# Narrower Q, K weight loads, joined rest loads and a re-ordered first stage in a conditioned attention and MLP block

## The chip, the cores and the metric

The kernel runs on one core of one Trainium2 chip. The metric is device microseconds of one execution, the median of the runs shown. TensorE (PE) multiplies matrices, VectorE (DVE), ScalarE (ACT) and GpSimd (POOL) do elementwise work, and SyncE (SP) issues nearly all DMAs. A DMA is carried out by 16 DMA engines; in this text the row of work that waits at one of them is called a ring.

## The reference, cut to what matters

```
def _A_ref(x, wqkv, wo):                 # S 2048, D 448, H 16, Dh 28
    qkv = (x @ wqkv).reshape(B, S, 3, H, Dh).transpose(2, 0, 3, 1, 4)
    ...                                   # each position attends to 8 positions, 2 apart, back from itself
    return o.transpose(0, 2, 1, 3).reshape(B, S, D) @ wo
def _B_ref(x, w1, b1, w2, b2):           # F 1792
    y = _layernorm(x)
    return gelu(y @ w1 + b1) @ w2 + b2
mod = (silu(c) @ w_mod).reshape(1, 6, 1, -1)
sa, ca, ga, sb, cb, gb = (mod[:, i] for i in range(6))
h = _layernorm(x) * (1 + ca) + sa
x = x + ga * _A_ref(h, wqkv, wo)
h = _layernorm(x) * (1 + cb) + sb
x = x + gb * _B_ref(h, w1, b1, w2, b2)
```

All inputs are bf16. `c` has 448 numbers, `w_mod` is 448 by 2688, `wqkv` 448 by 1344.

## The kernel before, in words

The 2048 tokens lie in eight tiles of 256 (128 partitions, two tokens each), `x_all[:, p]`. The depth 448 is cut into three full k-tiles of 128 rows and a **rest** of 64 rows. A rest uses half of the PE's rows, so the kernel keeps two copies or two halves of each rest weight, one on partitions 0 to 63 and one on 64 to 127, and loads them with two DMAs of 64 rows: `wm_r` (rest of the modulation's columns for `sa` and `ca`), `wqr_st` (rest of the Q and K weights, twice the same rows) and the last k-tile of `Wv` (rest of V, twice the same rows).

The first stage runs so. PE multiplies dummy weights (`warm_w`) while the first loads come. `c` is spread over partitions, silu is made from it (`e_c`, `silu_bf`, then a broadcast copy `silu_bc`), and PE multiplies `wm_st`, `wm_r` and `wm_d` (a copy of columns of both, laid twice) with it; two DVE additions make `mod_col`. Meanwhile tile 0 is normalised (`zy`) and transposed on PE (`ptr`), and `hT` is made of `ptr` and `mod_col`. The loaded Q and K weights are spread from 28 to 32 columns per head by copies on ACT, DVE and POOL (`Wqk` for the three k-tiles, `Wqr` for the rest), and PE forms Q and K of tiles 0 and 1 from `hT`, `Wqk` and `Wqr`: first what the full k-tiles give, then the rest. `spread` reads 4 columns past the last head, so the loads before are 900 columns wide (2 D + 4).

Tiles 2 to 7 go another way ("turns"): their `zy` is transposed by DMA (`zT`), and their Q and K are formed in natural order straight from `wqk_st` and `wqr_st`. Then come attention in 9 batches, the output projection, the second normalisation and the MLP, with attention and MLP interleaved in three phases. The second part of the modulation (`wmod`, four loads, 1.5 MB in all) is needed by the PE product `pb`, from which the output projection's scale comes.

Every task has a number; the string `ORDER` lists the numbers in the order in which the instructions are written, which is the order on each engine and on SP's queue, with `:A`, `:D`, `:P` where another engine than the usual one takes it and `+n@m` for n dummy products. `SLOTS` gives the buffers. SP issues the DMAs in program order with eight semaphores in turn, so each issue also waits for the DMA eight before it.

Of the kernel before, what the change touches and what calls it, by code (L numbers as in the profile page):

```python
# [66 lines left out]
487 401 490 454 403 402 436 453 455 370 444 404 434 371:D 456 372 491 457 488 405 459 493 458 460 445 492 435 494 461  # L67
# [86 lines left out]
def kernel(  # L154
# [68 lines left out]
    silu_bf = cst.tile([128, KT], BF16, name="silu_bf")  # L223
# [11 lines left out]
    wqk_st = sb("hm", [128, KT - 1, 2 * D + HP - DH], BF16, "wqk_st")  # L235
    wqr_st = sb("h2", [128, 2 * D + HP - DH], BF16, "wqr_st")
# [9 lines left out]
    def dconst(us, fn, writes):  # L246
        early.append(add("DVE", us, fn, writes=writes, after=[one], name="const " + writes[0]))
# [22 lines left out]
    dconst(0.06, lambda: nc.vector.memset(neg_half[:], -0.5), ["neg_half"])  # L270
# [83 lines left out]
    load_rest(0)  # L354
    load_rest(1)
    load_x(2, 4)
# [30 lines left out]
    def c_cols():  # L387
# [8 lines left out]
    add("DVE", 0.08, lambda: nc.vector.tensor_tensor(out=silu_bf[:], in0=e_c[:], in1=psc.t[:, 0, 0:128 * KT:128], op=ALU.mult),  # L396
        reads=["e_c"], bufs=[psc], writes=["silu"], name="silu")
    add("ACT", 0.18, lambda: nc.scalar.copy(out=silu_bc[:], in_=silu_bf[:].unsqueeze(2).to_broadcast([128, KT, HP])),
        reads=["silu"], writes=["silu_bc"], name="silu_bc")
# [32 lines left out]
    def spread(half):  # L432
# [3 lines left out]
        for ks in [[k] for k in range(KT - 1)]:  # L436
            k0, n = ks[0], len(ks)
            dst, src = (lambda k0=k0, n=n: Wqk[:, k0:k0 + n, half]), (lambda k0=k0, n=n: heads(wqk_st.t[:, k0:k0 + n, half * D:half * D + D], H))
            add("DVE", 0.06 + 0.18 * n, lambda dst=dst, src=src: nc.vector.tensor_copy(out=dst(), in_=src()), reads=[f"wqk{k}" for k in ks],
                bufs=[wqk_st], writes=[f"W{half}{k}" for k in ks], port=True, name="spread",  # L440
                alt={"ACT": (0.13 + 0.43 * n, lambda dst=dst, src=src: nc.scalar.copy(out=dst(), in_=src())),
                     "POOL": (0.1 + 0.5 * n, lambda dst=dst, src=src: nc.gpsimd.tensor_copy(out=dst(), in_=src()))})

        for a in range(2):
            rows, c0 = slice(KS * a, KS * a + KS), half * D + a * D // 2
            src = lambda rows=rows, c0=c0: heads(wqr_st.t[rows, c0:c0 + D // 2], H // 2)
            add("DVE", 0.22, lambda rows=rows, src=src: nc.vector.tensor_copy(out=Wqr[rows, half], in_=src()), reads=[f"wr{a}"],
                bufs=[wqr_st], writes=[f"Wr{half}{a}"], port=True, name="spread r",
                alt={"ACT": (0.33, lambda rows=rows, src=src: nc.scalar.copy(out=Wqr[rows, half], in_=src())),
                     "POOL": (0.4, lambda rows=rows, src=src: nc.gpsimd.tensor_copy(out=Wqr[rows, half], in_=src()))})  # L450
# [4 lines left out]
    def stats(src, w, b, reads, bufs=()):  # L455
        add("DVE", 0.53, lambda: nc.vector.bn_stats(out=stt[:, w, b, 0:6], in_=src()), reads=reads, bufs=bufs, after=early if w == b == 0 else (),  # L456
# [506 lines left out]
```

## Time and profile before

| | |
|---|---|
| median of 3 runs | 168.64 us (167.93 to 169.38) |
| the profiled execution's own time | 169.75 us |
| its span | 168.1 us |
| busy PE, DVE, ACT, POOL | 161.5, 115.8, 102.7, 47.7 us |
| mean granted clock of TensorE | 1.00 |

The page counts an engine busy from the start of an instruction to its end, and matmul ends are modelled. The chain that ended last is followed back from the last instruction to what released each step. "Landing" of a DMA is the time from its issue until its semaphore shows all data there. Times in the views are from the span's start.

### The profile page before, as it was taken

Reading aid. Unit: us, or ns where it says so; the run is one execution under the profiler, and the core shown is the slowest. Engines: PE = TensorE matmul, PEld = TensorE weight load, DVE = VectorE, ACT = ScalarE, POOL = GpSimd, SP = SyncE. Lnnn points to the kernel's source line nnn. Section 1 sums busy time; section 2 is a strip of 40 time slices with the busy share of each in tenths; the row PEclk is TensorE's granted clock in tenths of the full one; section 3 lists DMA queues with packets and bytes.
Section 4 is the critical chain, followed back from the end, with each engine's and each line's share of the span. In section 5 each row is a group of like instructions: output and inputs, shape, how many; then the busy total and the mean of one; then the engine's idle time right before and its main releaser. Section 6 shows DMA issues by size and latency. Waiting matters only on the chain.

```text
span 168.1 us, 4962 instructions
## 1 busy us (share of the span) xinstructions
PE 161.5 (96%) x2126; PEld 83.4 (50%) x2126; DVE 115.8 (69%) x271; ACT 102.7 (61%) x142; POOL 47.7 (28%) x76
## 2 busy tenths in 40 slices
PE   7989989999997999999999999999999999999992
PEld 4768544345544544435565444556434455444562
DVE  6869899879899689998738877474798930400032
ACT  3368987779489954759866376956627730097300
POOL 4135252300361201269300113820003870007200
PEclk9999999999999999999999999999999999999999
DMA  5999989799997999910091000008110027110003
GB/s 153 325 335 297 168 265 134 152 201 170 221 200 182 236 150 236 169 35 0 4 139 46 4 0 0 4 0 97 35 55 0 0 43 195 49 60 0 0 0 109
DMA packets 35574, 18.78 MB, mean 112 GB/s; under 512 B 28508, under 2 KB 34593, under 8 KB 35553
## 3 DMA queue, kind: packets, MB, share of 16 engines
q1 hardware_dynamic: 35548, 18.47, 53.0%
q8 instruction: 16, 0.26, 0.7%
q14 instruction: 6, 0.04, 0.1%
q10 hardware_dynamic: 4, 0.00, 0.0%
HBM read 9.81 MB, written 1.84 MB: 69 GB/s over the span
## 4 chain that ended last, share of the span: by engine, by line
PE 81%; DMA 10%; DVE 2%; POOL 2%; issue 1%; SPq 1%; ACT 1%; POOLq 0%; DVEq 0%
PE p L883 26%; PE p L548 22%; PE pw L803 7%; PE pq L548 6%; PE p L554 4%; DMA x_all<-in_A_x_dram 4%; PE po L771 3%; PE lt L738 3%; PE pv L706 3%; PE pv L548 3%; DMA wm_st<-in_w_mod_dram 3%; DMA zT<-zy 2%; DMA kT<-zy 2%; PE pq L554 1%; PE pd L760 1%
## 5 line engine op out<-in xcount | busy, mean ns | idle before, releaser
L864 ACT ACTIVATE hm<-p,b_col 128x512 bf16<-128x512 f32 x56 | 33.9, 692 | 29.9 <-PE p L554 27.3
L883 PE MATMUL p<-w_s,hm 128*128 128x448 bf16 (+1 forms) x238 | 44.1, 342 | 0.0
L548 PE MATMUL p<-yT,w_s 128*128 128x512 bf16 x168 | 38.1, 379 | 0.0
L469 POOL TENSOR_TENSOR rs_all<-mvs,neg_half 128x2 f32<-128x2 f32 x22 | 16.7, 766 | 57.9 <-DVE mvs L458 57.8
L883 PEld LDWEIGHTS <-hm 128*128 128x128 bf16 x238 | 22.7, 98 | 19.2 <-issue 0.8
L889 DVE TENSOR_TENSOR x_all<-p,x1p 128x896 bf16<-128x896 f32 (+2 forms) x10 | 8.9, 902 | 25.9 <-PE p L883 25.9
L548 PEld LDWEIGHTS <-w_s 128*128 128x128 bf16 x168 | 15.8, 98 | 20.9 <-issue 2.9
L456 DVE BATCH_NORM_STATS2 stt<-x_all 128x6 f32<-128x448 bf16 x32 | 18.7, 610 | 1.2 <-DMA x_all<-in_A_x_dram 1.0
L745 ACT ACTIVATE et<-lt 128x928 bf16<-128x928 f32 x18 | 16.1, 947 | 5.3 <-PE lt L738 5.1
L841 POOL TENSOR_TENSOR x1p<-x_all,gbb_bc 128x448 f32<-128x448 bf16 x16 | 17.8, 1134 | 0.0
L548 PE MATMUL pq<-wqk_st,hT 128*128 128x448 bf16 x72 | 15.2, 354 | 0.6 <-DVE hT L502 0.5
L788 DVE TENSOR_TENSOR qT<-po,den 128x912 bf16<-128x912 f32 x9 | 9.9, 1104 | 7.0 <-ACT den L782 5.6
L751 DVE TENSOR_TENSOR et<-et,mask 128x928 bf16<-128x928 bf16 x18 | 11.6, 672 | 2.4 <-ACT et L745 2.4
L803 PE MATMUL pw<-wo_s,qT 128*128 128x448 bf16 x64 | 13.2, 353 | 0.0
L780 ACT ACTIVATE den<-pd 128x928 f32<-128x928 f32 x9 | 8.5, 940 | 5.8 <-PE pd L760 5.7
L819 DVE TENSOR_TENSOR h<-h,mod_bc 128x896 bf16<-128x896 bf16 x16 | 11.1, 709 | 0.3
L548 PEld LDWEIGHTS <-hT 128*128 128x128 bf16 x72 | 6.4, 98 | 7.7 <-issue 1.3
L628 ACT CAST zy<-pq 128x896 bf16<-128x896 f32 x10 | 9.0, 906 | 2.0 <-PE pq L554 1.9
L810 DVE TENSOR_TENSOR x_all<-pw,x_all 128x896 bf16<-128x896 f32 x8 | 8.7, 1088 | 1.7 <-PE pw L803 1.5
L782 ACT ACTIVATE den<-den,den_bias 128x928 f32<-128x928 f32 x9 | 9.6, 1072 | 0.2
L478 DVE TENSOR_SCALAR zy<-h,mvs,rs_all 128x448 bf16<-128x448 bf16 x16 | 6.6, 456 | 4.4 <-POOL rs_all L469 4.3
L456 DVE BATCH_NORM_STATS2 stt<-h 128x6 f32<-128x448 bf16 x16 | 9.4, 613 | 0.2
(115 smaller groups left out, 183.4 us busy)
## 6 DMA issues: line engine op xcount, KB each, us to landing
w_s<-in_B_w_dram SPq DMA_DIRECT2D x7, 224.0 KB, 4.2
out_dram<-x_all SPq DMA_DIRECT2D x7, 224.0 KB, 2.2
x_all<-in_A_x_dram SPq DMA_DIRECT2D x3, 448.0 KB, 6.0
wmod<-in_w_mod_dram SPq DMA_DIRECT2D x3, 448.0 KB, 7.0
w_s<-in_B_w_dram SPq DMA_DIRECT2D x3, 448.0 KB
wqk_st<-in_A_wqkv_dram SPq DMA_DIRECT2D x3, 225.0 KB
wm_st<-in_w_mod_dram SPq DMA_DIRECT2D x1, 672.0 KB
x_all<-in_A_x_dram SPq DMA_DIRECT2D x2, 224.0 KB, 2.6
```

The lines of the kernel that those rows point to most:

```text
L456: add("DVE", 0.53, lambda: nc.vector.bn_stats(out=stt[:, w, b, 0:6], in_=src()), reads=reads, bufs=bufs, after=early if w == b == 0 else ( ...
L469: ways = {"POOL": (0.55 + 0.17 * n, lambda: nc.gpsimd.tensor_tensor(out=r, in0=v, in1=neg_half[:, 0:n], op=ALU.pow))}
L548: nc.tensor.matmul(out(), lhsT=lhs(kt, slice(0, 128)), rhs=rhs(kt, slice(0, 128)), start=first and kt == 0, stop=not first and kt == KT - 2)
L745: exps.append(add("ACT", 0.83, lambda half=half, lt=lt: nc.scalar.activation(out=et.t[:, 2 * half:2 * half + 2].rearrange("p r m c -> p r ...
L751: nc.vector.tensor_tensor(out=ev, in0=ev, in1=mask[:], op=ALU.mult)
L782: exps.append(add("ACT", 0.96, lambda: nc.scalar.activation(out=den.t[:], in_=den.t[:], func=ACT.Exp, scale=-1.0, bias=den_bias[:]), bufs= ...
L788: nc.vector.tensor_tensor(out=qT[:, :, LEAD + q00:LEAD + q00 + 2 * WQ], in0=po.t[:, :, 0:NS * 4 * WQ].rearrange("p j (m c) -> p m j c", c=WQ),
L803: nc.tensor.matmul(pw.t[:, s, 0:D], lhsT=qT[:, KT * s + ft, LEAD + 128 * p:LEAD + 128 * p + 128], rhs=wo_s[:, ft, :], start=(ft == 0), sto ...
L819: add("DVE", 0.55, lambda vec=vec, op=op: nc.vector.tensor_tensor(out=h2.t[:], in0=h2.t[:], in1=vec.unsqueeze(1).to_broadcast([128, NS, D] ...
L841: add("POOL", 1.0, lambda n=n: nc.gpsimd.tensor_tensor(out=x1p.t[:, n, :], in0=xn(p, n), in1=gbb2_bc[:], op=ALU.add), reads=[f"x{p}", "gbb ...
L864: gelus.append(add("ACT", 0.585, lambda f=f, a=a, p1=p1s[g]: nc.scalar.activation(out=hm.t[:, f].rearrange("p n c -> p (n c)"), in_=p1.t[: ...
L883: nc.tensor.matmul(p2.t[:, n, 0:c1 - c0], lhsT=hm.t[:, f, n, q * 128:(q + 1) * 128], rhs=w2_s[:, f, c0:c1], start=(f == parts[0][0]), stop ...
```

## The change: what it does

Six things change together, and `ORDER` and `SLOTS` are new.

1. The Q and K weight loads are 896 columns wide instead of 900; the staging tiles are 928 wide, and two memsets on DVE clear the 4 columns behind the data.
2. Each pair of rest loads becomes one DMA with 128 destination partitions, whose source is named with an extra outermost step of count 2.
3. Tiles 2 and 3 of the tokens come in two loads of one tile each.
4. `silu_bc` is made in one DVE instruction instead of a DVE product and an ACT copy.
5. The four `wmod` loads stand behind the first two `zT` transposes in SP's queue instead of partly ahead of them.
6. The first stage is re-ordered on all engines, up to about the first output projection; from there on the engines have the same order as before.

```diff
+    def both(src, n):
+
+        return bass.AP(src.tensor, src.offset, [[n, 2], *src.ap])
-    def load_rest(a):
-        load(lambda a=a: nc.sync.dma_start(out=wqr_st.t[KS * a:KS * a + KS, :], in_=A_wqkv[(KT - 1) * 128:D, 0:2 * D + HP - DH]),
-             0.5, [f"wr{a}"], bufs=[wqr_st])
+    def load_rest():
+        load(lambda: nc.sync.dma_start(out=wqr_st.t[:, 0:2 * D], in_=both(A_wqkv[(KT - 1) * 128:D, 0:2 * D], 0)),
+             0.5, ["wr0", "wr1"], bufs=[wqr_st])
...
-        for a in range(2):
-            load(lambda a=a: nc.sync.dma_start(out=Wv[KS * a:KS * a + KS, KT - 1, :], in_=A_wqkv[(KT - 1) * 128:D, 2 * D:3 * D]),
-                 0.2, [f"wvr{a}"])
+        load(lambda: nc.sync.dma_start(out=Wv[:, KT - 1, :], in_=both(A_wqkv[(KT - 1) * 128:D, 2 * D:3 * D], 0)), 0.3, ["wvr0", "wvr1"])
...
-    for v in range(2):
-        load(lambda v=v: nc.sync.dma_start(out=wm_r.t[KS * v:KS * v + KS, :], in_=w_mod[(KT - 1) * 128:D, v * D:v * D + D]),
-             0.25, [f"wmr{v}"], bufs=[wm_r])
+    load(lambda: nc.sync.dma_start(out=wm_r.t[:], in_=both(w_mod[(KT - 1) * 128:D, 0:D], D)), 0.4, ["wmr0", "wmr1"], bufs=[wm_r])
...
-    load_x(2, 4)
+    load_x(2, 3)
+    load_x(3, 4)
...
-    add("DVE", 0.08, lambda: nc.vector.tensor_tensor(out=silu_bf[:], in0=e_c[:], in1=psc.t[:, 0, 0:128 * KT:128], op=ALU.mult),
-        reads=["e_c"], bufs=[psc], writes=["silu"], name="silu")
-    add("ACT", 0.18, lambda: nc.scalar.copy(out=silu_bc[:], in_=silu_bf[:].unsqueeze(2).to_broadcast([128, KT, HP])),
-        reads=["silu"], writes=["silu_bc"], name="silu_bc")
+    add("DVE", 0.2, lambda: nc.vector.tensor_tensor(
+        out=silu_bc[:], in0=e_c[:].unsqueeze(2).to_broadcast([128, KT, HP]),
+        in1=psc.t[:, 0, :].rearrange("p (k n) -> p k n", n=128)[:, :, 0:HP], op=ALU.mult),
+        reads=["e_c"], bufs=[psc], writes=["silu_bc"], name="silu_bc")
```

**SP's queue, first loads.** Before, from the first load on:

```order
L339 DMA x_all<-in_A_x_dram 128x896
L346 DMA wm_st<-in_w_mod_dram 128x3x896
L349 DMA wm_r<-in_w_mod_dram 64x448 x2
L339 DMA x_all<-in_A_x_dram 128x896
L325 DMA wqk_st<-in_A_wqkv_dram 128x900
L329 DMA wqr_st<-in_A_wqkv_dram 64x900 x2
L325 DMA wqk_st<-in_A_wqkv_dram 128x900 x2
L339 DMA x_all<-in_A_x_dram 128x2x896 x2
L333 DMA Wv<-in_A_wqkv_dram 128x3x448
L335 DMA Wv<-in_A_wqkv_dram 64x448
L339 DMA x_all<-in_A_x_dram 128x2x896
L362 DMA wmod_274<-in_w_mod_dram 128x1792
```

and now:

```order
L345 DMA x_all<-in_A_x_dram 128x896
L352 DMA wm_st<-in_w_mod_dram 128x3x896
L354 DMA wm_r<-in_w_mod_dram 128x1x448
L345 DMA x_all<-in_A_x_dram 128x896
L329 DMA wqk_st<-in_A_wqkv_dram 128x896 x3
L337 DMA wqr_st<-in_A_wqkv_dram 128x1x896
L345 DMA x_all<-in_A_x_dram 128x896 x2
L341 DMA Wv<-in_A_wqkv_dram 128x3x448
L342 DMA Wv<-in_A_wqkv_dram 128x1x448
L345 DMA x_all<-in_A_x_dram 128x2x896 x2
L531 DMA_TRANSPOSE zT<-zy_98 128x8x128
L531 DMA_TRANSPOSE zT<-zy_99 128x8x128
```

The shapes are those of the destination. The joined loads have 128 rows there; tiles 2 and 3 stand behind all of `wqk_st` and `wqr_st`, and the first `zT` turns stand where the first `wmod` load stood.

**DVE, around silu and the modulation.** Before, from the first half of tile 0's normalisation on:

```order
L478 TENSOR_SCALAR zy_96<-x_all,mvs,rs_all 128x448
L396 TENSOR_TENSOR silu_bf<-e_c,ps_c 128x4
L418 COPY wm_d<-wm_st 128x6x64 x2
L478 TENSOR_SCALAR zy_96<-x_all,mvs,rs_all 128x448
L265 MEMSET add_col 128x4
L266 MEMSET add_col 128x4
L418 COPY wm_d<-wm_r 128x64 x2
L488 COPY zy_96<-zy_96 128x2x64
L456 BN_STATS stt<-x_all 128x6 x2
L425 TENSOR_TENSOR mod_col<-ps_col,add_col 128x8
```

and now, from its second half on:

```order
L482 TENSOR_SCALAR zy_96<-x_all,mvs,rs_all 128x448
L422 COPY wm_d<-wm_st 128x6x64
L399 RECIPROCAL e_c<-e_c 128x4
L422 COPY wm_d<-wm_r 128x64 x2
L422 COPY wm_d<-wm_st 128x6x64
L492 COPY zy_96<-zy_96 128x2x64
L400 TENSOR_TENSOR silu_bc<-e_c,ps_c 128x128
L460 BN_STATS stt<-x_all 128x6 x2
L462 BN_AGGR mvs<-stt 128x2 x2
L429 TENSOR_TENSOR mod_col<-ps_col,add_col 128x8
```

The last step of silu, which stood ahead of the copies out of `wm_r`, now stands behind them.

**POOL, the copies of Q and K weights.** Before, after its last memset of `zy`:

```order
L442 COPY Wqk_72<-wqk_st_156 128x512
L450 COPY Wqr_73<-wqr_st_176 64x256
L469 TENSOR_TENSOR rs_all_110<-mvs_109,neg_half_91 128x2
L450 COPY Wqr_73<-wqr_st_176 64x256
L469 TENSOR_TENSOR rs_all_110<-mvs_109,neg_half_91 128x2 x2
```

and now, at the same place:

```order
L284 MEMSET mask1_90 128x58
L287 AFFINE_SELECT mask1_90<-mask1_90 64x58
L289 AFFINE_SELECT mask1_90<-mask1_90 64x58
L287 AFFINE_SELECT mask1_90<-mask1_90 64x58
L289 AFFINE_SELECT mask1_90<-mask1_90 64x58
L446 COPY Wqk_72<-wqk_st_125 128x512 x2
L454 COPY Wqr_73<-wqr_st_127 64x256
L446 COPY Wqk_72<-wqk_st_125 128x512
L454 COPY Wqr_73<-wqr_st_127 64x256 x2
```

POOL now has three of the four `Wqr` copies, with one `Wqk` copy standing behind the first of them, and the reciprocal roots of tiles 1 to 3 (`rs_all`) have gone to ACT. ACT has the fourth `Wqr` copy, ahead of its four `hT` of tile 1.

More of the change, by code (lines that the diff above doesn't have):

```diff
@@ L222 @@
     e_c = cst.tile([128, KT], FP32, name="e_c")
-    silu_bf = cst.tile([128, KT], BF16, name="silu_bf")
     silu_bc = cst.tile([128, KT, HP], BF16, name="silu_bc")
@@ L234 @@
     wm_d = sb("h2", [128, 2 * KT - 1, 2 * KS], BF16, "wm_d")
-    wqk_st = sb("hm", [128, KT - 1, 2 * D + HP - DH], BF16, "wqk_st")
-    wqr_st = sb("h2", [128, 2 * D + HP - DH], BF16, "wqr_st")
+    wqk_st = sb("hm", [128, KT - 1, 2 * D + HP], BF16, "wqk_st")
+    wqr_st = sb("h2", [128, 2 * D + HP], BF16, "wqr_st")
     wmod2 = sb("hm", [128, KT, 4 * D], BF16, "wmod2")
@@ L244, with dconst @@
     early = []
-    def dconst(us, fn, writes):
-        early.append(add("DVE", us, fn, writes=writes, after=[one], name="const " + writes[0]))
+    def dconst(us, fn, writes, bufs=()):
+        early.append(add("DVE", us, fn, writes=writes, bufs=bufs, after=[one], name="const " + writes[0]))
     def const(us, fn, writes, reads=()):
@@ L269, with make_half @@
     add("DVE", 0.12, make_add, writes=["add_col"], after=[one], name="add_col")
-    dconst(0.06, lambda: nc.vector.memset(neg_half[:], -0.5), ["neg_half"])
+    def make_half():
+        nc.vector.memset(neg_half[:], -0.5)
+        nc.vector.memset(wqk_st.t[:, :, 2 * D:2 * D + HP - DH], 0.0)
+        nc.vector.memset(wqr_st.t[:, 2 * D:2 * D + HP - DH], 0.0)
+    dconst(0.2, make_half, ["neg_half", "wqpad"], [wqk_st, wqr_st])
     def pads():
@@ L317, in load @@
     def load(fn, us, writes, bufs=(), reads=(), fills=()):
-        queue.append(add("SP", 0.5, fn, reads=reads, writes=writes, bufs=bufs, fills=fills, after=queue[-1:] if len(queue) < 4 else queue[3:4], xfer=us,
+        queue.append(add("SP", 0.5, fn, reads=reads, writes=writes, bufs=bufs, fills=fills, after=queue[-1:] if len(queue) < 3 else queue[2:3], xfer=us,
                          name="load " + writes[0]))
@@ L324, in load_qk @@
     def load_qk(kt):
-        load(lambda: nc.sync.dma_start(out=wqk_st.t[:, kt, :], in_=A_wqkv[kt * 128:kt * 128 + 128, 0:2 * D + HP - DH]), 0.62, [f"wqk{kt}"],
+        load(lambda: nc.sync.dma_start(out=wqk_st.t[:, kt, 0:2 * D], in_=A_wqkv[kt * 128:kt * 128 + 128, 0:2 * D]), 0.62, [f"wqk{kt}"],
              bufs=[wqk_st])
-    def load_rest(a):
-        load(lambda a=a: nc.sync.dma_start(out=wqr_st.t[KS * a:KS * a + KS, :], in_=A_wqkv[(KT - 1) * 128:D, 0:2 * D + HP - DH]),
-             0.5, [f"wr{a}"], bufs=[wqr_st])
+    def both(src, n):
[3 more added lines that the diff above has]
+             0.5, ["wr0", "wr1"], bufs=[wqr_st])
     def load_wv():
         load(lambda: nc.sync.dma_start(out=Wv[:, 0:KT - 1, :], in_=rows128(A_wqkv[0:(KT - 1) * 128, 2 * D:3 * D])), 1.15, ["wv"])
-        for a in range(2):
-            load(lambda a=a: nc.sync.dma_start(out=Wv[KS * a:KS * a + KS, KT - 1, :], in_=A_wqkv[(KT - 1) * 128:D, 2 * D:3 * D]),
-                 0.2, [f"wvr{a}"])
+        load(lambda: nc.sync.dma_start(out=Wv[:, KT - 1, :], in_=both(A_wqkv[(KT - 1) * 128:D, 2 * D:3 * D], 0)), 0.3, ["wvr0", "wvr1"])
     def load_x(p0, p1):
@@ L353 @@
     load_x(1, 2)
[L354 to L356 removed]
+    load_rest()
+    load_x(2, 3)
+    load_x(3, 4)
     load_wv()
@@ L438, in spread @@
             dst, src = (lambda k0=k0, n=n: Wqk[:, k0:k0 + n, half]), (lambda k0=k0, n=n: heads(wqk_st.t[:, k0:k0 + n, half * D:half * D + D], H))
-            add("DVE", 0.06 + 0.18 * n, lambda dst=dst, src=src: nc.vector.tensor_copy(out=dst(), in_=src()), reads=[f"wqk{k}" for k in ks],
+            add("DVE", 0.06 + 0.18 * n, lambda dst=dst, src=src: nc.vector.tensor_copy(out=dst(), in_=src()), reads=["wqpad"] + [f"wqk{k}" for k in ks],
                 bufs=[wqk_st], writes=[f"W{half}{k}" for k in ks], port=True, name="spread",
@@ L446, in spread @@
             src = lambda rows=rows, c0=c0: heads(wqr_st.t[rows, c0:c0 + D // 2], H // 2)
-            add("DVE", 0.22, lambda rows=rows, src=src: nc.vector.tensor_copy(out=Wqr[rows, half], in_=src()), reads=[f"wr{a}"],
+            add("DVE", 0.22, lambda rows=rows, src=src: nc.vector.tensor_copy(out=Wqr[rows, half], in_=src()), reads=["wqpad", f"wr{a}"],
                 bufs=[wqr_st], writes=[f"Wr{half}{a}"], port=True, name="spread r",
@@ L455, in stats @@
     def stats(src, w, b, reads, bufs=()):
-        add("DVE", 0.53, lambda: nc.vector.bn_stats(out=stt[:, w, b, 0:6], in_=src()), reads=reads, bufs=bufs, after=early if w == b == 0 else (),
+        add("DVE", 0.53, lambda: nc.vector.bn_stats(out=stt[:, w, b, 0:6], in_=src()), reads=reads, bufs=bufs,
             writes=[f"st{w}_{b}"], name="stats")
```

38 lines of the change are left out of this document (19 added, 19 removed), and 24 rows, old and new, of tables (ORDER, SLOTS).

## The prediction

> **What bounds the kernel now.** I read the page's busy times first, then windows by stage, then the chain that ended last, then the first stage's timeline.
>
> ```profile
> span 168.1 us, 4962 instructions
> PE 161.5 (96%) x2126; PEld 83.4 (50%) x2126; DVE 115.8 (69%) x271; ACT 102.7 (61%) x142; POOL 47.7 (28%) x76
> ```
>
> ```profile
> core 0: us, PE busy (x) PEld busy (x) DVE busy (x) ACT busy (x) POOL busy (x), PEclk, DMA share, GB/s
> 9.20:12.00 2.80, 2.37 (x25) 1.78 (x23) 1.79 (x7) 1.70 (x5) 1.09 (x2) 1.00 0.97 336
> 12.00:22.80 10.80, 10.22 (x215) 6.75 (x214) 9.45 (x28) 9.83 (x14) 5.03 (x11) 1.00 0.95 250
> 22.80:34.00 11.20, 10.83 (x186) 4.93 (x189) 10.06 (x24) 8.20 (x12) 3.17 (x4) 1.00 0.91 167
> 46.00:52.00 6.00, 5.15 (x98) 2.41 (x99) 5.83 (x16) 5.32 (x7) 2.75 (x3) 1.00 1.19 159
> 64.00:110.00 46.00, 46.00 (x598) 22.12 (x598) 36.00 (x75) 31.55 (x44) 17.32 (x21) 1.00 0.30 54
> ```
>
> PE is the bound: from 64 to 110 us it does not pause, and from 9.2 to 64 its pauses are few: 0.43, 0.58, 0.37 and 0.85 us in the windows above. So a delay of PE's first real products travels to the end, less what it takes back of these pauses; and an improvement of the first stage can earn little more than the pauses that it closes. Until then the DMAs set the pace (share 0.97 in 9.2 to 12 us), as the chain shows:
>
> ```profile
> 1.26 4.57 DMA wm_st<-in_w_mod_dram
> ...
> 6.32 6.00 DMA x_all<-in_A_x_dram
> 12.34 1.68 DVE stt L456 x3
> ...
> 17.56 3.38 DMA zT<-zy
> ...
> 21.04 1.71 DVE hT L502 x3
> ```
>
> The first modulation load lands at 5.83 us (1.26 + 4.57). Tiles 2 and 3, issued at 6.32, land at 12.32: six microseconds in the rings' queues, where the first tile, with nothing ahead, took 2.6.
>
> **How a DMA is dealt to the rings.** This decides what a joined load costs.
>
> ```profile
> q10 hardware_dynamic: 4, 0.00, 0.0%
> c_row<-in_c_dram ACTq DMA_DIRECT2D x1, 0.9 KB
> c_row<-in_c_dram ACTq DMA_DIRECT2D x1, 0.1 KB
> ```
>
> ```profile
> q1 hardware_dynamic: 576, 0.46, 27.3%
> out_dram<-x_all SPq DMA_DIRECT2D x1, 224.0 KB
> out_dram<-x_all SPq DMA_DIRECT2D x2, 56.0 KB
> out_dram<-x_all SPq DMA_DIRECT2D x1, 112.0 KB, 1.7
> ```
>
> Of the whole run (first rows) queue 10 carries only the two loads of `c`, one row each, and has 4 packets: a row of data and one packet that ends it, for each. The others are the window 163 to 168.05 us, the last four stores of 128 rows each: 576 packets are 512 rows and 64 more, 16 for each store. I read the additional packets as one for each ring that took part: a DMA of one row runs on one ring, a DMA of 128 rows on all 16. The outermost count deals the work out.
>
> The joined loads have 128 at the destination, but 2 at the source (`[[n, 2], *src.ap]` in the diff). I take the smaller count: **two rings**, 64 rows each. The Trainium skill speaks against this change in the same direction. "DMA: Bandwidth & Descriptors", section "Rules for kernel authors", says that an outermost dimension smaller than 16, such as a leading zero-stride broadcast, confines the whole DMA to at most that many engines; by that rule the time is my forecast, and if the destination's 128 decided, it would be the first rival. No DMA of this run has unequal counts on its two sides, so no row here settles it.
>
> **The change part by part.**
>
> *Joined loads.* The sizes and the pace of a ring:
>
> ```profile
> wm_r<-in_w_mod_dram SPq DMA_DIRECT2D x2, 56.0 KB, 4.3
> wqr_st<-in_A_wqkv_dram SPq DMA_DIRECT2D x2, 112.5 KB, 4.5
> x_all<-in_A_x_dram SPq DMA_DIRECT2D x2, 224.0 KB, 2.6
> GB/s 0 0 0 70 274 225 342 407 385 395 323 340 255 288 255 331 303 306 329 358 347 339 362 372 381 411 401 372 130 127 78 133 185 81 244 210 263 128 101 365
> ```
>
> The window 9.2 to 12 gives 336 / 0.97 / 16 = 21.6 GB/s for a busy ring; the best slice of the first 22 us (411) gives 25.7. Between the two I take the mean, 23.6 GB/s. A joined `wm_r` puts 56 KB on each of two rings: 2.43 us, where sixteen rings need 0.30. A joined `wqr_st` puts 112 KB there: 4.86 us instead of 0.61. `Wv`'s rest costs 2.43 again, but is needed only past 20 us. On these two rings the queue now runs: `wm_st` lands at 5.83; `wm_r` at 5.83 + 2.43 = 8.26 (before: issue 1.73 + 4.3 = 6.0); tile 1 and three `wqk_st`, each 14 KB for a ring, 4 x 0.61 = 2.43; `wqr_st` at 8.26 + 2.43 + 4.86 = **15.55**. Before:
>
> ```profile
> 6.00 0.15 DVE L396 TENSOR_TENSOR silu_bf<-e_c,ps_c 128x4 bf16<-128x4 f32 x1
> 6.19 0.30 ACT L398 COPY silu_bc<-silu_bf 128x128 bf16<-128x128 bf16 x1 [0.61 <-DVE silu_bf L396]
> 7.62 0.61 POOL L442 COPY Wqk<-wqk_st 128x512 bf16<-128x512 bf16 x1 [5.07 <-DMA wqk_st<-in_A_wqkv_dram]
> 8.59 0.56 ACT L504 ACTIVATE hT<-ptr,mod_col 128x256 bf16<-128x256 bf16 x1 [0.39 <-DVE mod_col L425]
> 8.71 0.40 POOL L450 COPY Wqr<-wqr_st 64x256 bf16<-64x256 bf16 x1 [0.48 <-DMA wqr_st<-in_A_wqkv_dram]
> 10.44 0.39 ACT L449 COPY Wqr<-wqr_st 64x256 bf16<-64x256 bf16 x1
> 12.04 0.61 PE L554 MATMUL pq<-hT,Wqr 64*128 64x256 bf16 x8
> 22.79 2.25 PE L548 MATMUL pq<-wqk_st,hT 128*128 128x448 bf16 x11 [0.54 <-DVE hT L502]
> ```
>
> The first half of `wqr_st` was there by 8.71. Behind the wait for it POOL now holds a `Wqr` copy, a `Wqk` copy and two more `Wqr` copies: 15.55 + 0.40 + 0.61 + 0.40 + 0.40 = 17.36. PE's last products of tile 0's rest need the last copy, half of the eight being done by then: they end at about 17.6, not at 12.65 (12.04 + 0.61): **+4.95 us**. ACT has a `Wqr` copy and then four `hT` of tile 1 (0.40 + 4 x 0.56 behind 15.55, and in them a wait for tile 2's statistics); tile 1's products start on the first three, so PE loses nothing more there.
>
> *What it takes back.* The 0.58 us of PE's pauses from 12 to 22.8 go: 0.54 of them was the wait for `hT` of tiles 2 and 3 in the last row, which will be there (next paragraph). The pauses at 33 and 51 us hang on the same turns and stay: net +4.4.
>
> *Tiles 2 and 3 apart.* They stand behind `wqr_st` and land at 16.2 and 16.8 on the two rings, later than the 12.32 of before. From landing to `hT` took 22.75 - 12.32 = 10.4 us: 27.2 at the latest. PE asks for it at 22.79 + 4.4, and 1.6 us later since a third group of V products now stands ahead: 28.8. Hidden, with 1.6 to spare. The DVE order no longer holds POOL's mask building in this path, so it is shorter, not longer.
>
> *One-step silu.* Two steps of 0.15 and 0.30, ended at 6.49, become one, between 0.15 and 0.45 by these rows; I take 0.3. But it stands behind the copies out of `wm_r` on DVE, so it starts at 8.26 plus four small copies, about 9.0. PE's modulation products wait for it, and `hT` of tile 0 moves from 8.59 to about 11.2. The full k-tiles' products of tile 0 then run from 11.3 and have time until 16.5: hidden by the wait for `wqr_st`. Were that wait gone and this one left, it would cost up to 2.6.
>
> *Narrower loads, memsets.* In 5.6 to 9.2 us, when the 900-column rows ran, a ring made 298 / 1.05 / 16 = 17.7 GB/s:
>
> ```profile
> 5.60:9.20 3.60, 3.51 (x56) 2.79 (x55) 3.40 (x18) 1.52 (x4) 1.02 (x3) 1.00 1.05 298
> ```
>
> At 21.6 the four loads' 57 KB for a ring take 2.65 instead of 3.2 us: a gain between 0 and 0.6, contained in the pace that I used. Two memsets on DVE cost 0 to 0.1, off the path.
>
> *Second modulation loads behind two turns.* SP reaches them after the second turn, at about 22 instead of 9.5, and every DMA that is issued there, seven with `wo_s`, goes past the queue in 4 to 5 us. The last landed 5.8 us after its issue at 20.45; 26 + 5.8 gives 31.8 where `pb` asks for it at 27.0 + 4.4 and a little more. Cost 0 to 1.0; I take 0, since the rings are empty by then.
>
> Sum: the profiled execution took 169.75 us, 1.7 more than its span; +4.4 gives 174.1. The median of the runs is 168.64, so I forecast **173.0 us**. At 25.7 GB/s the rest of tile 0 ends at 16.8 (+4.15, net 3.6: 172.2); at 21.6 it ends at 18.5 (+5.8, net 5.2: 173.9), with the late modulation 174.9. The forecast's own range is 171.5 to 175.
>
> **The rivals.**
>
> *Sixteen rings (faster or the same).* If the destination's 128 rows deal a joined load out, `wm_r` costs 0.30 and `wqr_st` 0.61 on a ring, as two halves do now, and SP saves three issues. Tiles 2 and 3 land about 1 us sooner, and the turns no longer stand behind 672 KB of `wmod`. PE can then close the pauses that wait on these: 0.43 + 0.58 + 0.37 = 1.4, less 0.3 for silu behind the copies: 167.5, from 166.3 to 168.6. For it: the two halves of before did go well as separate DMAs of 64 rows. Against: the outermost count of the source is 2. It decides if a ring's end packets number 16 for a joined load.
>
> *Two rings, mostly hidden.* Lone rings may run faster than a sixteenth of 411 GB/s, and PE may take back the pauses at 33 and 51 us too (0.37 + 0.85): 172.2 less 1.2, less up to 1 for a faster pace: 170 to 171.5. Against: a ring at 9 tenths busy leaves little.
>
> *The change as meant, and lost at PE.* Sixteen rings, but PE's pauses are only moved: 168.6.
>
> **How the numbers follow.** Two rings at full cost 0.75 (171.5 to 175.5), two rings mostly hidden 0.08, sixteen rings with a gain 0.10, sixteen without 0.07. The range 167.5 to 175.2 leaves out some 0.08 at each end. About 1% (1.7 us) is what a measurement of this kernel can tell from no change. Faster by over that, below 166.9, needs all pauses closed: 0.05. Within: 0.17, the sixteen rings' rest. Slower: 0.78.
>
> **What would show each step.** Right: `wm_r` landing near 8.3 and `wqr_st` near 15.5 after issues near 1.7 and 4.2; a wait of POOL's `Wqr` copy on `wqr_st` of some 4 us; PE's first `Wqr` products near 17, with pauses of several microseconds between 11 and 17; PE without pause behind. Wrong: `wqr_st` landing before 10, or PE's rest of tile 0 starting before 13; then the rings were sixteen and the time lies below 169.

## Result and the profile after

The changed kernel takes **176.43 us** (median of 4 runs, 175.67 to 176.79), the kernel before 169.01 (167.93 to 169.68): ratio **1.0434, 95% interval 1.0377 to 1.0491**. The prediction was 173.0 (167.5 to 175.2), and the time lies outside that range. The direction and the two rings came as written; the loss is 3.4 us larger, because the prediction never asked when the load of tiles 4 and 5 lands, and a path through it was longer than the forecast's own. Executions in a slower state that some of these kernels fall into now and then are left out of the ratios; in the run `s_queue` below they were five of ten, so its time is given by its ratio. The profiled execution took 176.57 us, its span is 174.9. From the page of the changed kernel (span, busy times, DMA packets, the engines' shares of the chain):

```profile
span 174.9 us, 4946 instructions
PE 161.9 (93%) x2119; PEld 84.2 (48%) x2119; DVE 116.5 (67%) x272; ACT 103.4 (59%) x148; POOL 45.3 (26%) x73
q1 hardware_dynamic: 35474, 18.47, 48.9%
PE 72%; DMA 18%; DVE 5%; SPq 2%; issue 1%; ACT 0%; DVEq 0%; ACTq 0%
```

and the same two last rows of the kernel before:

```profile
q1 hardware_dynamic: 35548, 18.47, 53.0%
PE 81%; DMA 10%; DVE 2%; POOL 2%; issue 1%; SPq 1%; ACT 1%; POOLq 0%; DVEq 0%
```

PE is busy for as long as before (161.9 and 161.5), so nearly all of the 6.8 us of span are pauses of PE, and the DMAs' share of the chain has gone from 10% to 18%. The packets answer the question of the rings. Six DMAs of 64 rows went, each with 16 end packets (-96), three joined ones came, and tiles 2 and 3 are one DMA of 128 rows more (+16). 35548 - 96 + 16 leaves 35468; the page has 35474, six more: **two end packets for each joined load, two rings**.

The windows of the changed kernel, from 9 us on (first column the stretch, then its length and PE's busy time):

```profile
core 0: us, PE busy (x) PEld busy (x) DVE busy (x) ACT busy (x) POOL busy (x), PEclk, DMA share, GB/s
9.20:12.00 2.80, 2.80 (x46) 2.42 (x46) 2.21 (x9) 2.09 (x6) 1.16 (x2) 0.50 0.64 210
12.00:18.00 6.00, 3.50 (x33) 2.30 (x32) 2.84 (x11) 2.24 (x5) 2.44 (x5) 0.96 0.52 160
26.00:30.00 4.00, 2.34 (x82) 1.37 (x81) 3.00 (x11) 3.05 (x4) 0.91 (x2) 1.00 0.94 281
34.00:40.00 6.00, 4.67 (x102) 2.45 (x98) 4.20 (x10) 4.32 (x8) 0.57 (x1) 1.00 1.11 165
```

The pause of 2.5 us from 12 to 18 was forecast. The 1.66 us from 26 to 30 and the 1.33 us from 34 to 40 were not, and neither was a granted clock of 0.50 from 9.2 to 12. Instruction by instruction (start, duration, engine; in brackets the wait ahead and what ended it):

```profile
8.34 0.27 DVE L422 COPY wm_d<-wm_r 128x64 bf16<-128x64 bf16 x2 [0.48 <-DMA wm_r<-in_w_mod_dram]
8.78 0.28 DVE L400 TENSOR_TENSOR silu_bc<-e_c,ps_c 128x128 bf16<-128x128 f32 x1
15.43 0.39 POOL L454 COPY Wqr<-wqr_st 64x256 bf16<-64x256 bf16 x1 [4.73 <-DMA wqr_st<-in_A_wqkv_dram]
16.44 0.39 PE L566 MATMUL pq<-hT,Wqk 128*128 128x256 bf16 x2 [2.50 <-POOL Wqk L446]
16.76 0.87 PE L558 MATMUL pq<-hT,Wqr 64*128 64x256 bf16 x8
20.96 0.63 DVE L460 BATCH_NORM_STATS2 stt<-x_all 128x6 f32<-128x448 bf16 x1 [1.37 <-DMA x_all<-in_A_x_dram]
21.50 0.69 DVE L482 TENSOR_SCALAR zy<-x_all,mvs,rs_all 128x448 bf16<-128x448 bf16 x2
27.76 1.64 PE L710 MATMUL pv<-Wv,hT 128*64 128x448 bf16 x16 [1.66 <-ACT hT L508]
```

`wm_r` is there at 8.3 (forecast 8.26), `wqr_st` at 15.4 (15.55), PE's rest of tile 0 ends at 17.63 (17.6). Then come the surprises. Until 20.96 DVE waits 1.37 us for the load of tiles 4 and 5: their statistics stand in its order ahead of the normalisation of tile 3 (21.50). So tile 3's transpose starts late. `hT` is made for tiles 2 and 3 together, so tile 2's is late with it, and PE waits for it at its third V group. The chain that ended last, from 8 to 47 us, holds just these steps (rows under 1.35 us are left out):

```profile
8.80 1.35 SPq L342
10.20 10.74 DMA x_all<-in_A_x_dram
...
22.49 4.38 DMA zT<-zy
32.63 5.14 DMA zT<-zy
...
42.16 4.50 DMA zT<-zy
```

Tiles 4 and 5 took 10.74 us from issue to landing, behind `wqr_st` and the rest of `Wv` on the two rings. No row of the chain is the load of `wqr_st` or PE's wait for it; it counts here only as part of what stood ahead on the two rings. The forecast's own path, from `wqr_st` to PE, was no longer the longest.

### The profile page after: what moved, and what is told of

Same layout as the page of the kernel before. It is cut to its first block, busy times and chain, and to the rows that moved or that the text cites. A ratio compares the mean times of both kernels' runs of the same rounds, so it can differ in the third digit from the quotient of the medians.

```text
span 174.9 us, 4946 instructions
## 1 busy us (share of the span) xinstructions
PE 161.9 (93%) x2119; PEld 84.2 (48%) x2119; DVE 116.5 (67%) x272; ACT 103.4 (59%) x148; POOL 45.3 (26%) x73
## 3 DMA queue, kind: packets, MB, share of 16 engines
q1 hardware_dynamic: 35474, 18.47, 48.9%
## 4 chain that ended last, share of the span: by engine, by line
PE 72%; DMA 18%; DVE 5%; SPq 2%; issue 1%; ACT 0%; DVEq 0%; ACTq 0%
PE p L887 25%; PE p L552 21%; DMA x_all<-in_A_x_dram 10%; DMA zT<-zy 8%; PE pw L807 7%; PE p L558 4%; PE pq L552 3%; PE pv L552 3%; PE lt L742 3%; PE po L775 2%; PE pv L710 2%; DVE qT L792 1%; DVE zy L482 1%; PE pd L764 1%; DVE hT L506 1%
## 5 line engine op out<-in xcount | busy, mean ns | idle before, releaser
L473 POOL TENSOR_TENSOR rs_all<-mvs,neg_half 128x2 f32<-128x2 f32 x19 | 14.3, 754 | 63.3 <-DVE mvs L462 63.3
L893 DVE TENSOR_TENSOR x_all<-p,x1p 128x896 bf16<-128x896 f32 (+2 forms) x10 | 8.9, 902 | 26.1 <-PE p L887 26.1
L807 PE MATMUL pw<-wo_s,qT 128*128 128x448 bf16 x64 | 13.2, 353 | 0.1
L710 PE MATMUL pv<-Wv,hT 128*64 128x448 bf16 (+1 forms) x80 | 8.0, 360 | 1.7 <-ACT hT L508 1.7
```

Source lines behind the costliest of these rows:

```text
L473: ways = {"POOL": (0.55 + 0.17 * n, lambda: nc.gpsimd.tensor_tensor(out=r, in0=v, in1=neg_half[:, 0:n], op=ALU.pow))}
L710: nc.tensor.matmul(pv.t[WK * j:WK * j + WK, s, 0:D], lhsT=hT[rows, NS * kt + s, kc + j * WQ:kc + j * WQ + WK], rhs=Wv[rows, kt, :], start= ...
L807: nc.tensor.matmul(pw.t[:, s, 0:D], lhsT=qT[:, KT * s + ft, LEAD + 128 * p:LEAD + 128 * p + 128], rhs=wo_s[:, ft, :], start=(ft == 0), sto ...
```

## The experiments

Ratios are to the kernel before, run beside each experiment on the same chip, with 95% intervals.

### The joined loads undone, all and one by one

```diff
-    load(lambda: nc.sync.dma_start(out=wm_r.t[:], in_=both(...)), ...)
+    load(lambda: [nc.sync.dma_start(out=wm_r.t[KS * v:KS * v + KS, :], in_=...) for v in range(2)], ...)
```

and alike for `wqr_st` and the rest of `Wv`: two DMAs of 64 rows from one entry of the order, nothing else moved.

> The changed kernel with each of the three joined rest loads issued as two DMAs of 64 rows again; all else of the change stays (narrower loads, tiles 2 and 3 apart, one-step silu, late second modulation loads, new order). Theory (the joined loads run on two rings and this is the whole loss): wqr_st is there by about 9, PE's rest products of tile 0 end by 13, the queue's end packets rise again by 90 (from 35474 packets to 35564), and the time is 167 to 169 us against 169.0 of the kernel before and 176.4 of the changed one. Rival (the new order and the late second modulation loads carry a good part of the loss): 171 us or more, with PE still waiting between 26 and 40 us.

Measured: **170.97 us, ratio 1.0100 (1.0067 to 1.0134)**. The rings cost 5.46 us of the change (176.43 - 170.97). Without them I had expected 167 to 169, no loss at all; what is left is a loss of 1%.

```profile
q1 hardware_dynamic: 35564, 18.47, 50.8%
```

The packets are 35548 + 16: with halved loads the six are gone. PE's longest waits behind the start of the program (what waited, for whom; us in total, times, the longest):

```profile
PE ps_col L414 <- DVE silu_bc L400: 1.1, 1, 1.1
PE pq L552 <- DVE qT L792: 1.0, 1, 1.0
PE pb L645 <- DMA wmod<-in_w_mod_dram: 0.9, 1, 0.9
```

The first hangs on the copies that now stand ahead of silu. The other two are gone in `s_wmod` below, where the second modulation loads go back.

> The changed kernel with only the Q, K rest load split in two DMAs of 64 rows; wm_r and Wv's rest stay joined. Theory: two rings lose 4.3 us of queue, so wqr_st lands at about 11.3 instead of 15.4 and PE's rest products of tile 0 end near 14.5 instead of 17.6; Wv's rest still delays tiles 4 to 7 by 2.4. The time is 172 to 174 us. Rival (what counts is how many joined loads are left, not their bytes): a third of the loss comes back, 174.0.

Measured: 173.33, ratio 1.0242 (1.0178 to 1.0307), the time that I expected: `wqr_st` carries 3.1 us of the rings' 5.5. The way there was another: PE's clock was 0.50 from 9.2 to 12 us, and the rest of tile 0 ended at 16.4, not near 14.5. The rival's 174.0 lies inside the interval; it falls by the next two runs, neither of which gives a third back.

> The changed kernel with only the rest of Wv split in two DMAs of 64 rows. PE's rest products of tile 0 are untouched by it (17.6). Theory A (the additional loss behind them comes from tiles 4 and 5, which land late behind Wv's rest while their statistics stand ahead of tile 3's normalisation on DVE): the second turn is issued at 21 instead of 22.5, PE's wait for hT at 27.8 shrinks from 1.7 to below 0.6, and the time is 174.5 to 175.3 us. Theory B (the additional loss comes from the second modulation loads ahead of the third and fourth turn): unchanged, 176.0 to 176.6.

Measured: 177.02, ratio 1.0438 (1.0363 to 1.0514), unchanged. In its trace DVE no longer waits for tiles 4 and 5 and starts `hT` of tiles 2 and 3 at 25.67 instead of 26.97, as it should if the rest of `Wv` makes tiles 4 and 5 late. But PE now waits 3.5 us for the spread weights, and its chain runs through `wqr_st`:

```profile
4.36 12.25 DMA wqr_st<-in_A_wqkv_dram
```

It landed at 16.61 instead of 15.38 in this execution, though it is issued ahead of what was edited, and PE then ran tile 1's 24 products at half clock (4.46 us instead of 2.92). So PE came to its third V group too late to wait for any `hT`: the run shows that tiles 4 and 5 made `hT` late, and not what their lateness alone cost.

> The changed kernel with only wm_r split in two DMAs of 64 rows. Theory: wm_r lands at 6 instead of 8.3, PE's modulation products start at about 7.2 instead of 9.1, and everything behind in the two rings comes 2.1 us earlier: wqr_st at 13.2, PE's rest of tile 0 ends at 15.5, the time is 173.8 to 174.8 us. Rival (silu behind wm_r's copies is the bound, not wqr_st's queue): PE's first product of hT and Wqk comes 2 us earlier but its rest of tile 0 does not, and the time stays above 175.5.

Measured: 175.61, ratio 1.0354 (1.0274 to 1.0434): 0.8 us, less than expected and not clear of noise. `wqr_st` landed at 14.2 and not 13.2, and the rest of tile 0 ended at 16.5, 1.1 us sooner than in the changed kernel. Singly the three loads give back 3.9 us at most, together 5.5: they stand behind each other.

### The joined loads alone, in the kernel before

```diff
+    def both(src, n):
+        return bass.AP(src.tensor, src.offset, [[n, 2], *src.ap])
-    for a in range(2): dma_start(out=wqr_st.t[KS * a:KS * a + KS, :], in_=...)
+    dma_start(out=wqr_st.t[:], in_=both(..., 0))        # likewise wm_r and the rest of Wv
```

> The kernel before with the three joined loads alone (each as one DMA with the outer step of count 2, at the place of the first of the two it replaces); everything else as before. Theory A (a joined load runs on two rings and what needs it waits; nothing else in the change matters by itself): wm_r lands near 8.3, then tile 1 and one wqk_st (1.2 us), wqr_st near 14.3, the other two wqk_st near 15.6; the last Q, K products of tile 0 near 17, 4.5 us late: 173 to 175. Rival B (the change's new order and later modulation loads cost as much as the rings do): 170.5 to 172.5, since this kernel's order hides part of the wait. If the two rings were not the cause at all: 169.

Measured: **177.06, ratio 1.0493 (1.0436 to 1.055)**, more than either theory gave. One part of the change, done alone, costs as much as all of it (0.6 us more, within the intervals): here `wqr_st` stands ahead of two `wqk_st`, which then wait for it. PE's two pauses:

```profile
8.40 0.24 PE L414 MATMUL ps_col<-silu_bc,wm_r 64*128 64x32 bf16 x6 [1.87 <-DMA wm_r<-in_w_mod_dram]
...
15.88 0.91 PE L566 MATMUL pq<-hT,Wqk 128*128 128x256 bf16 x4 [2.52 <-DVE Wqk L443]
```

and its granted clock behind the second (0.50, the last number but two of the window):

```profile
18.00:22.80 4.80, 4.80 (x31) 3.11 (x30) 3.65 (x13) 2.94 (x5) 2.75 (x8) 0.50 0.66 210
```

Behind both pauses PE runs at half its clock for a while (0.52 from 9.2 to 12 us). That opened a new question.

### Is the half clock part of the loss?

Dummy products with zero weights fill PE's two long pauses (`+n@m` in the order, and 20 that add zeros to an open sum):

```diff
-60+15@60
+60+37@60
+FILL = {93: (20, 91)}        # 20 products of warm_w ahead of task 93
```

> The changed kernel with 42 more dummy products of zeros on PE, 22 while it waits for silu_bc (2.7 us) and 20 while it waits for the rest weights (2.5 us), so that it is busy through its two long pauses and its granted clock stays at 1.00 (it was 0.97 to 0.99 over the run, 0.50 from 10 to 12 us). Theory A (the clock is not on the path, since PE waits for wqr_st and then for tiles 2 and 3 whatever its clock): 176 to 176.8. Rival B (the half clock costs the 2.4 us beyond the prediction): 174 to 175.

Measured: 176.44, ratio 1.0480 (1.0408 to 1.0552). In three of the four runs the clock was 0.997 or more, and these took 176.27 to 176.54: **unchanged. In the changed kernel nothing is won by restoring the clock**, so it is not on the path, unless the dummy products cost elsewhere what it won; only the fourth run has a trace (177.94, with the clock still at half from 12 to 15.4 us). Its chain has the same step as the changed kernel's:

```profile
12.02 10.90 DMA x_all<-in_A_x_dram
```

The same in the kernel before with joined loads (15 and 20 more dummy products):

> The kernel before with the three joined loads alone (177.06), with 35 more dummy products of zeros on PE in its two long pauses (1.9 us for wm_r, 2.5 us for the spread of wqk_st), which leave its granted clock at 1.00 instead of 0.50 from 9 to 12 and 16 to 23 us. Theory A (there the half clock is on the path: its first real products took 10 us instead of 7): 173.5 to 175, the rest of tile 0 ending near 18 instead of 20.2. Rival B (DMAs alone set the pace there): 176.5 to 177.3.

Measured: 176.00, ratio 1.0435 (1.0376 to 1.0495), 1.06 us less than without (all four runs lie below all four, though the ratios' intervals overlap): there the clock seems to be on the path, for a third of what I gave it. The rest of tile 0 still ended at 20.03, not near 18; the gain came in tile 1's products, which ended 0.8 us sooner. One pause of 1.93 us was left, and the clock fell once more:

```profile
15.90 0.71 PE L569 MATMUL pq<-hT,Wqk 128*128 128x256 bf16 x4 [1.93 <-DVE Wqk L446]
```

```profile
18.00:22.80 4.80, 4.80 (x38) 3.28 (x36) 3.87 (x13) 3.27 (x6) 2.71 (x8) 0.64 0.63 205
```

### Tiles 2 and 3 ahead of the slow load

```diff
 # SP's queue in the changed kernel
-wqk_st x3, wqr_st, x_all (tile 2), x_all (tile 3), Wv
+wqk_st x3, x_all (tile 2), x_all (tile 3), wqr_st, Wv
```

> The changed kernel (176.4) with one thing moved: the loads of tiles 2 and 3 stand ahead of the joined wqr_st in SP's queue, instead of behind it. Theory A (what the prediction missed is tiles 2 and 3: they land behind the two slow rings, their hT comes at 27 to 28, and PE waits 1.66 us for it): tiles 2, 3 land 3 to 4 us sooner, wqr_st 0.6 to 1.2 later, PE's wait of 1.66 goes, and the time falls by 0.5 to 1.5 us: 175 to 175.9. Rival B (PE's half clock after its pauses is what was missed): wqr_st later, nothing won: 176.5 to 177.5.

Measured: 177.48, ratio 1.0522 (1.0458 to 1.0586). The wait for `hT` of tiles 2 and 3 went, as theory A has it; the time is rival B's:

```profile
18.30 0.61 PE L566 MATMUL pq<-hT,Wqk 128*128 128x256 bf16 x2 [3.58 <-POOL Wqk L446]
...
19.81 4.78 PE L552 MATMUL pq<-hT,Wqk 128*128 128x256 bf16 x24
```

PE waits 3.58 us instead of 2.50 for the weights that POOL copies behind `wqr_st`, and then runs tile 1's 24 products at half clock, 4.78 us where the changed kernel took 2.92. Both together:

> The changed kernel with both: tiles 2 and 3 ahead of the joined wqr_st (alone 177.48) and dummy products of zeros in PE's two long pauses (alone 176.44): 22 while it waits for silu_bc, 30 while it waits for the rest weights. Theory A (tiles 2, 3 and the half clock stand side by side behind the late wqr_st, and taking one away only shows the other): the clock stays near 1.00, PE has no wait for hT of tile 2, tile 1's Q, K products take 3.0 us instead of 4.8: 174.5 to 175.7. Rival B (what is beyond the prediction lies elsewhere, behind 30 us): 176.2 to 177.5.

Measured: 179.23, ratio 1.0609 (1.0565 to 1.0654), against both theories. The first stage went as theory A said (clock 1.00, no wait for tile 2, the 24 products in 2.79 us), and PE began the first output projection at 47.42, 0.6 us sooner than the changed kernel; the loss came later, as the shares of the chain and PE's waits show:

```profile
PE 69%; DMA 16%; ACT 5%; DVE 3%; issue 3%; POOL 1%; SPq 0%; DVEq 0%
```

```profile
PE p L890 <- issue: 1.0, 1, 1.0
PE p L555 <- DMA yT<-zy: 0.9, 1, 0.9
...
PE pw L810 <- issue: 0.8, 1, 0.8
```

3% of the chain is "issue", where the other runs have 0 to 2%: PE stood still at 48 and 96 us for nothing that the profile shows. Whether the 52 more dummy products bring that, and how, is open, so this run does not say what tiles 2 and 3 and the clock would be worth together.

### The 1% that halved loads leave

First two steps of the halved version's new order (170.97), moved by entries of the order:

```diff
 # s_wmod: SP's queue            # s_silu: DVE
-x_all (6, 7), zT, zT, wmod x2   -wm_d copies, tail of tile 0, silu_bc
+x_all (6, 7), wmod x2, zT, zT   +silu_bc, wm_d copies, tail of tile 0
```

> The changed kernel with all rest loads in two halves (as in the first experiment, 170.97), and with two of the four second modulation loads back ahead of the first two turns in SP's queue, right behind the last load of x. Theory A (the remaining 2 us are the late modulation loads: pb waits 0.9 us for them, and the turns of tiles 4 and 5 stand behind them): 168.8 to 169.5, pb's wait gone, zT of tiles 4, 5 landing before 31. Rival B (the remaining 2 us are the first stage, silu behind the copies): unchanged, 170.5 to 171.3, or slower if the first turns are now late.

Measured: 170.52, ratio 1.0114 (1.0024 to 1.0203): the wait of `pb` is gone, and the time is not better.

> The changed kernel with all rest loads in two halves, and with the one-step silu moved on DVE ahead of the copies of wm_st and wm_r and of tile 0's tail; nothing else moved. Theory A (the late modulation loads): unchanged, 170.6 to 171.3, since the 0.7 us won at 8 us is lost again at pb and at the turns. Rival B (the first stage): silu ends near 6.4 instead of 7.6, hT of tile 0 near 8.4 instead of 9.3, and the time falls by 0.7 to 1.2: 169.8 to 170.3.

Measured: 171.80, ratio 1.0181 (1.011 to 1.0253): no gain. But silu ended only 0.4 us sooner (7.20 instead of 7.63), and DVE's `hT` of tile 0 started at 9.35 in both, since statistics of the next tile stand ahead of `mod_col` on DVE. So the run does not clear the place of silu; it hardly changed it.

> The changed kernel with all rest loads in two halves, the modulation loads ahead of the turns as in the one experiment and silu ahead of the copies as in the other. Theory A and rival B each hold in part: 167.8 to 168.8, at or below the kernel before. If neither is the cause: 170.5 to 171.3, and the rest of the order must hold the 2 us.

Measured: 170.85, ratio 1.0151 (1.007 to 1.0231): the two steps as I moved them do not hold the 1%, singly or together. So I turned it round, and put the edits into the **old** order:

```diff
 # kernel before, its ORDER and halved loads kept
+896-column loads and memsets; silu_bc in one step; tiles 2 and 3 in two loads
```

> The kernel before, in its own order and with its rest loads in halves, with three of the change's edits: 896-column loads and the memsets, silu in one step (at the place of the first of its two), tiles 2 and 3 in two loads. Theory A (these edits are good or neutral, and the 1.0% that is left in the changed kernel without joined loads is its new order): 167.8 to 168.9. Rival B (one of these edits costs it): 169.8 to 171.

Measured: **168.23, ratio 0.9981 (0.9943 to 1.0019)**: these three edits cost nothing, and gain nothing that can be measured. It is the best version of the study, and no different from the kernel before. What the halved version loses against it, 2.7 us by the medians and 2.0 by the ratios, lies in the new order. SP's queue and the engines apart:

```diff
 # b_queue: old engines, SP's queue as changed      # s_queue: changed engines, SP's queue as before
-wqk_st, wqr_st x2, wqk_st x2, x_all ..., wmod x2, zT, zT
+wqk_st x3, wqr_st x2, x_all ..., zT, zT, wmod x2
```

> The kernel before with the three good edits and halved loads (168.23 in its own order), and with the change's order in SP's queue alone: wqr_st behind all of wqk_st, tiles 6 and 7 last, the second modulation loads behind two turns. Engines keep the order of before. Theory A (the queue's order holds the 2.7 us between 168.23 and the changed kernel with halved loads, 170.97): 170 to 171.5. Rival B (the engines' order holds it): 168 to 169.

Measured: 170.99, ratio 1.0111 (1.0068 to 1.0153): theory A.

> The changed kernel with halved loads (170.97) and the order of before in SP's queue: wqr_st behind the first wqk_st, tiles 6 and 7 ahead of Wv, two of the second modulation loads ahead of the turns. Engines keep the changed order. Theory A (queue): 168.2 to 169.3. Rival B (engines): 170.3 to 171.5.

Measured: ratio 1.0097 (1.0055 to 1.0140), some 170.5 us: rival B. Both answers together say that the parts are not a sum: either half of the new order, beside the other half of the old, costs what the whole new order costs. Last, SP's queue by its two steps, in the old order:

```diff
 # b_wmod_late: only "wmod x2" behind "zT, zT"      # b_first: only the loads ahead of them in the new order
```

> The kernel of the three good edits in the old order (168.23) with one step moved: two of the second modulation loads stand behind the first two turns, as in the change. Theory A (this step, which the prediction took at nothing, is where the queue's new order loses its 2.8 us: pb waits for the last load, and the turns of tiles 4 and 5 stand behind them): 170 to 171. Rival B (the order of the first loads costs it): 168 to 169.

Measured: **171.38, ratio 1.0142 (1.0088 to 1.0196)**: theory A, and the step that the prediction took at nothing. The rows are the turns of tiles 4 and 5 on SP's queue, PE's wait for the modulation, and DVE behind the turns:

```profile
24.14 5.40 SPq L533 DMA_TRANSPOSE zT<-zy  x2
...
29.63 0.67 PE L647 MATMUL pb<-wmod,silu_bc 128*32 128x448 bf16 x8 [1.33 <-DMA wmod<-in_w_mod_dram]
...
33.08 0.74 DVE L508 TENSOR_SCALAR hT<-zT,mod_col 128x512 bf16<-128x512 bf16 x2 [3.50 <-DMA zT<-zy]
```

Without that one step (`b_old_order`) the same two turns were issued in half the time:

```profile
23.44 2.60 SPq L533 DMA_TRANSPOSE zT<-zy  x2
```

The 0.7 us between the two starts are not the edit's: in this execution PE had already waited 1.5 us for `wm_r` at 7 us.

> The kernel of the three good edits in the old order (168.23) with the first loads in the change's order (wqr_st behind all of wqk_st, tiles 6 and 7 last), and the second modulation loads where they were, ahead of the turns. Theory A (late modulation loads hold the queue's 2.8 us): 168 to 169.2. Rival B (the first loads): 170 to 171.

Measured: 170.42, ratio 1.0103 (1.0048 to 1.0159): rival B too. PE waits for copies of weights, which the engines still take in the old order of the loads:

```profile
PE pq L568 <- ACT Wqk L447: 0.9, 1, 0.9
...
PE pq L568 <- DVE Wqk L445: 0.8, 1, 0.8
```

> The changed kernel (176.43), joined loads and all, with two of the second modulation loads back ahead of the first two turns in SP's queue. Theory A (late modulation loads): the turns of tiles 4 and 5 land 2 to 3 us sooner, the pauses from 30 to 40 us (1.55) go, 174.5 to 175.5. Rival B (in this order the place of these loads does not matter, as with halved loads, where 170.97 became 170.52): 176 to 177.

Measured: 178.55, ratio 1.0588 (1.0513 to 1.0662): both theories fall. In the joined kernel the early modulation loads make things worse by 2.1 us. The load of tiles 4 and 5 takes 1.3 us longer than in the changed kernel (10.74), and the turn behind it 0.5 longer (4.38):

```profile
10.29 12.06 DMA x_all<-in_A_x_dram
...
23.90 4.91 DMA zT<-zy
```

PE's wait for `hT` of tiles 2 and 3 grows from 1.66 to 1.95 us, behind products of tile 1 that ran at half clock (4.46 us). That the modulation loads share the rings with the late tiles would explain it; no run shows it apart. Late modulation loads are, in any case, not what the joined kernel lost beyond the prediction.

## Why the prediction was right, and where it was wrong

- **PE is the bound, and a delay of the first stage travels to the end**: right. PE's busy time is the same, and what was lost by 64 us is lost at the end. That PE would have no pause behind tile 0, which the prediction named as a sign of being right, did not come.
- **Two rings**: right, shown by the packets of three kernels: 35474 in the changed one; 35564 with halved loads; and in the kernel before with joined loads 35458, which is 35548 - 96 + 6.
- **"Joined loads", +4.95 us**: right as a term. `wqr_st` at 15.4 and the rest of tile 0 at 17.63 instead of 12.65: +4.98. Undoing them gains 5.46. That it matches within 0.2 us is in part luck: in `a_split_v`, which does not touch `wqr_st`, it landed at 16.61.
- **"`Wv`'s rest costs 2.43 again, but is needed only past 20 us"**: **this is the step that failed.** I asked when `Wv` itself is needed, and not what stands behind it on the same two rings. That is the load of tiles 4 and 5 (10.74 us to landing), and DVE's order has their statistics ahead of tile 3's normalisation: DVE waited 1.37 us there. The prediction has no term for this load, though its own pace would have given one: tile 3 at 16.8, then `Wv` 0.9, its rest 2.4 and tiles 4 and 5 1.2 make 21.3, where 20.94 was measured.
- **"Hidden, with 1.6 to spare"** (tiles 2 and 3): failed through that. Tiles 2 and 3 themselves landed about as forecast, and the path behind them was not shorter, as I wrote, but held DVE's new wait. My latest time for `hT`, 27.2, was near: ACT's part was there at 27.76. But PE asked at 26.1 (27.76 - 1.66), for the V group that I had counted as standing *ahead* of the request at 28.8: this V group already needs `hT` of tiles 2 and 3. The -0.58 of "What it takes back" became +1.66.
- **"The pauses at 33 and 51 us hang on the same turns and stay"**: of the two, the trace of before shows the first behind a transposed `kT` and the second behind nothing that the profile shows ("issue"), so the reading was a guess. The pauses grew. I expected 1.22 us of pauses to remain behind tile 0 (0.37 + 0.85); there are 3.31 from 18 to 64 us, 1.66 and 1.33 of them in the two windows above. These 2.1 us are most of what the sum missed: it gave 174.1 for a profiled execution, which took 176.57.
- **From the sum to the median**: I took 1.1 us off, since the profiled execution of before lay that far above the median. The changed kernel's lies 0.1 above its own. So 1.0 of the 3.4 us comes from carrying one execution's distance to the median over to another kernel.
- **"Second modulation loads behind two turns ... I take 0, since the rings are empty by then"**: wrong by itself (1.6% in the old order, from 0.9981 to 1.0142), and the trace shows what its own first sentence names: seven DMAs go between the turns, and the next turns are issued and land behind them. In the joined kernel it is not the cause of the miss.
- **"One-step silu", "Narrower loads, memsets"**: right as far as shown: PE's wait for `wqr_st` came behind them in the changed kernel, and in the old order they have no effect.
- **The rival with sixteen rings** was priced wrongly too: 167.5, while halved loads, which do run on sixteen rings, give 170.97. I had costed the new order at nothing and its pauses as closed.
- **The granted clock** is in no step of the prediction. It fell to 0.50 for a while, and that filling the pauses won nothing here is luck, not foresight.

Open: how the 2.1 us of pauses divide between the late tiles 4 and 5 and the turns. That tiles 4 and 5 made `hT` late is read from the traces; no run that shortened one path alone (`Wv`'s rest, tiles 2 and 3, the clock) became faster, and the run that took two of them away met a stall of another kind.

## What to carry to other kernels

Before two DMAs are joined, look at the outermost count on both sides: a count of 2 put 112 KB on each of two rings, and the three joined loads cost 5.5 us against halves of 64 rows. When a transfer gets slower, follow every transfer behind it on its rings, and from each the engine order that waits for it: the loss came through a load that the change does not touch. Here, with PE busy for 96%, the order fitted its queue as a whole: half of the new order cost as much as all of it. So try an edit in the old order first, one step at a time.

## What the runs showed of the hardware

- **SP took longer to issue a load behind one that puts much on two rings.** Two loads of `x`, in the changed kernel (the time that SP took to issue both, then the second alone) and before (both):

```profile
10.20 5.16 SPq L345 DMA_DIRECT2D x_all<-in_A_x_dram  x2
14.14 1.22 SPq L345 DMA_DIRECT2D x_all<-in_A_x_dram  x1
```

```profile
6.32 0.94 SPq L339 DMA_DIRECT2D x_all<-in_A_x_dram  x2
```

  The first of the two in the changed kernel, tiles 4 and 5, stands right behind the joined rest of `Wv` and took 3.90 us; with halved loads in the same order (`a_split_all`) it took 0.59. I read this as SP waiting for room on the two rings; the views do not show what it waits for. What stands behind in the queue starts later too: tiles 6 and 7 at 14.14, with halved loads at 10.27. Behind seven loads the same happened: one of the two turns in the 5.40 us above took 4.05.
- **A pause of PE of 1.87 us was followed by half the clock** (kernel before with joined loads: 0.52 in the window from 9.2 to 12 us), and one of 2.52 us by 0.50 from 18 to 22.8. The Trainium skill, "TensorE: Matmul & The Clock Gate", section "Part 1: The HAM clock gate", puts an idle window of about 3.4 us ahead of that; these traces show it after less. But not each such pause did it: after 2.50 us in the changed kernel the clock was 1.00 from 18 to 22.8. So the length of the pause alone does not decide; what else does is open. In `j_x23_fill`, whose dummy products left no pause over 0.8 us from 4 to 34 us, the clock was 1.00 all through.
